# Fused linear attention and MoE block on one core: MoE groups of four chunks, with the second weight stationary and the output kept transposed

## The chip, the core and the metric

The kernel runs on one core of one Trainium2 chip. The metric is device time in microseconds (us), from the launch of the one program to its end. Lower is better. The kernel before takes 521.38 us, the median of three runs (520.69 to 521.63). Arrays are rearranged on the host before and after the program; that is not in the time.

## The reference, cut to what matters

Two stages follow each other. The first is a linear attention with a decaying state, over 4 batches, 8 heads, 768 time steps and a head dimension of 48:

```
cur = (u * k_t) outer v_t
y_t = r_t @ (state + cur)
state = w_t * state + k_t outer v_t
```

Its output is read as `x`, 3072 tokens by 384. The second stage is a two-layer network with 2048 hidden units:

```
h = x @ w_in                                      # 3072 x 2048
g = max(h, 0) + alpha * min(h, 0)
out = g @ w_out                                   # 3072 x 384
```

Everything is single precision in and out. The weights arrive as 64-bit numbers and are turned into single precision on the chip.

## The kernel before, in words

**Chunks.** Time is cut into 12 pieces of 64 steps, and batches are taken in pairs, so there are 24 chunks of 128 tokens, q = 0 to 23. For each chunk VectorE (DVE) runs two scans over the decay `w` and scales `k` and `r`; TensorE (PE) forms scores, the output of the chunk and the update of the state in many 64x64 matmuls; the result goes to `x` in two parts, a rounded high part and the low remainder, so that three fast matmuls (high x high, high x low, low x high) give close to single precision. A quarter of the rows of `x` comes out on other partitions, in a tile `x3s`, and six small DMAs per group (L614) move it to its place.

**Weights.** There are 16 tiles of 128 hidden units, j = 0 to 15. Each tile is read from memory as 64-bit numbers (`raw<-in_wts_dram`, L647, 768 KB, into one of two `raw` buffers), put together by DVE (L659, L662, L666), split into `wh` and `wl`, and stays in SBUF. The tiles used in the first steps keep their `w_out` half whole at first; it goes to `wl` by a DMA (`wl<-cx`, L631).

**MoE steps.** Chunks are joined in groups of 2, 2, 3, 3, 3, 3, 3, 3 and 2 (`GROUPS`). One step is one group with one weight tile: `moe_up` (L691) issues 9 matmuls (three parts of K, three products) with 128 hidden units as stationary and the tokens of the group moving, 256 or 384 columns; ScalarE (ACT) and DVE make `g` from the sum (L697, L699) and split it into `gh` and `gl` (L704, L705); `moe_down` of the step two before (`LAG = 2`) then issues, for each chunk of the group, three matmuls with the chunk's 128 columns of `g` as stationary and 384 columns of `w_out` moving (L719). Each chunk has its own accumulator in PSUM, a tile `op`, of which there are three. In the first 24 steps `g` isn't split: one exact single-precision product (L713), which the chip runs as two passes, takes the place of the three.

**Order at the start.** Attention must yield chunks and the weights must be read before the matmuls can run. So the first two groups of two chunks take turns over the weight tiles: tiles 0 to 5 with group 0, then with group 1, then tiles 6 to 10 with each, then 11 to 15 with each (`PHASES`). When a group is left, its unfinished sums are written to memory (`part<-os`, L746), and read back and added by DVE (L735, L737) when it is taken up again.

**What sets the order.** All operations are first recorded with an engine, a duration, what they read and write, and a due time. A planner (`Plan.order`) then plays the engines forward and gives each the ready operation with the earliest due time; the program is emitted in that order, and each engine and SyncE's (SP) one DMA queue run it strictly in that order. `LEAD`, `UNIT`, `ATT`, `PLACE` and `PLACE_REST` set the due times: at which step each chunk's attention is wanted.

**The end.** When a group is done, the sums of each chunk are copied from PSUM to one of two `os` tiles by ACT or DVE (L743, L740) and written with two DMAs (L751). A check that the fast path was allowed runs beside it; its result, `flag`, is read by every engine before a branch.

Of the kernel before, what the change touches and what calls it, by code (L numbers as in the profile page):

```python
# [8 lines left out]
F32 = mybir.dt.float32  # L9
# [24 lines left out]
GT = 3 * P  # L34
# [14 lines left out]
LEAD = 22.0  # L49
UNIT = 1.05  # L50
ATT = 2.9

PLACE = {0: (-1, -1), 1: (4, 5)}
PLACE_REST = (12, 7, 3)
# [3 lines left out]
WHOLE_TO = 24  # L58
# [3 lines left out]
CHECK_FROM = 52  # L62
# [163 lines left out]
def fast_path(tc, wgt, flag, dmaj, nat, u, ud, vg, wts, alpha, out, part):  # L226
# [12 lines left out]
    with tc.tile_pool(name="const", bufs=1) as const, tc.tile_pool(name="psum", bufs=1, space=PSUM) as psum:  # L239
# [36 lines left out]
        r_x = ring("x", [P, 2, KT, GT], 3, F32R)  # L276
# [4 lines left out]
        r_os = ring("os", [P, DM], 2)  # L281
# [6 lines left out]
        def warm():  # L288
            return tmp.ap[:, 2 * P:]
# [32 lines left out]
        group, starts = [], []  # L322
        for g, size in enumerate(GROUPS):
            starts.append(len(group))
            group += [(g, i) for i in range(size)]
        begins, first, sizes = [], {}, []
        for g, j0, j1 in PHASES:
            first.setdefault(g, len(sizes))
            begins.append(len(sizes))
            sizes += [GROUPS[g]] * (j1 - j0)  # L330
        steps = len(sizes)
        before = {}
        for q, (g, i) in enumerate(group):
            before.setdefault(PLACE[g][i] if g in PLACE else first[g] - PLACE_REST[i], []).append(q)
# [3 lines left out]
        for i in range(steps + 5):  # L338
            for q in before.get(i, ()):
                due_att[q] = now  # L340
                now += ATT
            due_step.append(now)
            now += UNIT * (sizes[i] if i < steps else 3)

# [4 lines left out]
        def load(q):  # L349
# [11 lines left out]
            if q < GROUPS[0]:  # L361
                op("SP", 0.4, lambda: nc.sync.dma_start(out=extra[q].ap, in_=vg[q]), w=[extra[q]], lat=0.55)
# [101 lines left out]
        def outputs(q, nxt):  # L464
# [5 lines left out]
            g, s = group[q]  # L470
            size = GROUPS[g]
            kr, nv, at = ready.pop(q)
            ss = slice(s * P, (s + 1) * P)
            if s == 0:
                xs[g] = Tensor(r_x), Tensor(r_x3) if g > 0 else None
            x, xr = xs[g]
            yb = Tensor(r_op if g == 0 else bank), Tensor(bank)
# [13 lines left out]
            def own(same):  # L491
# [3 lines left out]
                for j in range(2):  # L495
                    for o, e in ORDER:
                        i, p = o if same else 1 - o, 2 * j + e
                        h = o * NP + p
                        if g > 0 or 2 * o + j < KT:
                            made.append(mm(yb[o], FULL[e], col(j, i), not same, lhsT=nv.ap[FULL[i], h * 64:(h + 1) * 64],  # L500
                                           rhs=at.ap[FULL[i], o, p, :]))
                if g == 0:
# [67 lines left out]
            if g == 0:  # L570
# [34 lines left out]
            take(g > 0)  # L605
            if g > 0 and nxt:
                rest()
            if g > 0 and s == size - 1:
                src = [(xr, (i, j, 1)) for i in range(size) for j in range(2)]
                old = [(x, (i, j, o)) for i in range(size) for j in range(2) for o in range(2)]  # L610
                for e in range(2):
                    for k in range(KT):
                        def move(r=64 * e + D, f=64 * e + 16 * k, k=k):
                            nc.sync.dma_start(out=x.ap[r:r + 16, :, k, 0:size * P].bitcast(F32), in_=xr.ap[f:f + 16, :, 0:size * P].bitcast(F32))  # L614
                        op("SP", 0.4, move, r=src + old, w=[(x, ("d", e, k))], lat=0.15)

        def x_keys(g):
            x = xs[g][0]
            return [(x, (i, j, o)) for i in range(GROUPS[g]) for j in range(2) for o in range(2)] + (
                [(x, ("d", o, k)) for o in range(2) for k in range(KT)] if g > 0 else [])  # L620


        whole = {j for i, (g, j0, j1) in enumerate(PHASES) for j in range(j0, j1) if begins[i] + j - j0 < WHOLE_TO}
# [19 lines left out]
        def weight_tile(j):  # L643
# [5 lines left out]
            for i0, i1 in ((0, 1), (1, 2)) if j < SPLIT else ((0, 2),):  # L649
# [15 lines left out]
                if j in whole:  # L665
# [15 lines left out]
        def moe_up(n, g, j, lag):  # L681
            x, w = xs[g][0], GROUPS[g] * P
            us = lambda t: t * (0.25 + 0.25 * GROUPS[g])
            hp, pos = Tensor(bank), Tensor(r_pos)

            def products():
                i = 0
                for k in range(KT):
                    ks = slice(k * P, (k + 1) * P)
                    for a, xi in ((wh, 0), (wl, 0), (wh, 1)):  # L690
                        nc.tensor.matmul(hp.ap[:, 0:w], lhsT=a[:, j, 0, ks], rhs=x.ap[:, xi, k, 0:w],  # L691
                                         start=(i == 0), stop=(i == 3 * KT - 1))
                        i += 1
            t = UNIT * GROUPS[g]
            op("PE", t / 2, products, r=[("wh", j, 0), ("wl", j, 0), ("down", n - lag - 1), *x_keys(g)], w=[hp, "up"], kind="MM",
               due=due_step[n] + t / 2 - (t if n == steps - 1 else 0))
            op("ACT", us(0.6), lambda: nc.scalar.activation(out=pos.ap[:, 0:w], in_=hp.ap[:, 0:w], func=AF.Relu, scale=alpha_n[:, j:j + 1]),  # L697
               r=[hp, "alpha"], w=[pos])
            op("DVE", us(0.58), lambda: nc.vector.scalar_tensor_tensor(  # L699
                out=pos.ap[:, 0:w], in0=hp.ap[:, 0:w], scalar=0.0, in1=pos.ap[:, 0:w], op0=ALU.max, op1=ALU.subtract), r=[hp], w=[pos])  # L700
            if n < WHOLE_TO:
                return pos, None
            gh, gl = Tensor(r_gh), Tensor(r_gl)
            op("ACT", us(0.54), lambda: nc.scalar.copy(out=gh.ap[:, 0:w], in_=pos.ap[:, 0:w]), r=[pos], w=[gh])  # L704
            op("DVE", us(0.6), lambda: nc.vector.tensor_tensor(out=gl.ap[:, 0:w], in0=pos.ap[:, 0:w], in1=gh.ap[:, 0:w].bitcast(F32), op=ALU.subtract),  # L705
# [3 lines left out]
        def moe_down(n, g, j, lag, gh, gl, j0, j1):  # L709
            size = GROUPS[g]  # L710
            for s in range(size):
                def whole_products(s=s):
# [359 lines left out]
```

## Time and profile before

| | |
|---|---|
| median of three runs | 521.38 us (520.69 to 521.63) |
| the profiled execution | 520.97 us, of which 519.2 us is the span of the trace |
| instructions in the span | 13761 |
| PE busy, DVE busy, ACT busy | 501.7 us, 345.6 us, 300.3 us |
| matmuls of `moe_up` | 1296 (864 + 432) |
| matmuls of `moe_down`, in three products | 1008 (3 x 336) |
| passes of exact `moe_down` | 96 |
| PE's granted clock, mean | 0.996 |

A row of the grouped view names line, engine, operation, output tile, then input tiles (the moving one first for a matmul), its shape and count, the busy time and the mean duration of one, and the idle time of the engine before them with what ended it. Matmuls overlap in their pipeline, so the duration of one (some 0.3 us) is longer than the spacing from one to the next; the spacing is read from the chain of waits, whose rows give start, length and number of a run of matmuls. Busy times of DVE and ACT count overlapping time once.

### The profile page before, as it was taken

The numbers are of one execution on the slowest core, as the hardware profiler recorded it, in microseconds if no ns is written. First come the engines' busy times: TensorE is split into PE (matmuls) and PEld (weight loads), VectorE is DVE, ScalarE is ACT, GpSimd is POOL, SyncE is SP. The second block draws the span as 40 slices with busy tenths as digits, with TensorE's granted clock in tenths as the row PEclk, the third lists the DMA queues.
The fourth block names the chain that finished last, engine by engine and source line by source line (L and its number), as shares of the span: only waits on it lengthen the run. The fifth ranks groups of instructions, "written<-read, shape, count | busy, mean of one in ns | idle before, by whom it ended". The sixth has DMA issues, their size and how long they took to land.

```text
span 519.2 us, 13761 instructions
## 1 busy us (share of the span) xinstructions
PE 501.7 (97%) x5654; PEld 473.4 (91%) x5654; DVE 345.6 (67%) x657; ACT 300.3 (58%) x806; POOL 74.4 (14%) x100
## 2 busy tenths in 40 slices
PE   9996899999999999999999999999999999999993
PEld 8984677789999999999999999999999999999992
DVE  6989798998888898768336665676753434433341
ACT  3765754865354576756555566676775656533441
POOL 2010120262001544213000210102000000000000
PEclk9999999999999999999999999999999999999998
DMA  8878768765231668465413556447461045000101
GB/s 300 277 263 286 235 237 283 257 204 151 78 104 33 220 197 271 121 194 157 113 59 103 177 159 208 139 145 228 126 227 61 15 120 180 7 12 16 33 1 37
DMA packets 31945, 78.27 MB, mean 151 GB/s; under 512 B 4480, under 2 KB 13184, under 8 KB 31872
## 3 DMA queue, kind: packets, MB, share of 16 engines
q1 hardware_dynamic: 31872, 77.30, 46.6%
q8 instruction: 46, 0.75, 0.6%
q14 instruction: 27, 0.22, 0.1%
HBM read 66.27 MB, written 6.29 MB: 140 GB/s over the span
## 4 chain that ended last, share of the span: by engine, by line
PE 85%; DMA 8%; DVE 3%; SPq 1%; ACT 1%; issue 1%; POOL 0%; DVEq 0%; POOLq 0%
PE bank L691 36%; PE op L719 32%; PE bank L483 5%; PE op L713 5%; DMA raw<-in_wts_dram 4%; DMA wl<-cx 3%; PE bank L440 2%; PE bank L458 1%; PE bank L527 1%; PE bank L758 1%; SPq L614 1%; PE bank L766 1%; PE bank L401 1%; DVE cx L662 0%; DVE cx L666 0%
## 5 line engine op out<-in xcount | busy, mean ns | idle before, releaser
L691 PE MATMUL bank<-x,wh 128*128 128x384 f32 (+1 forms) x864 | 230.2, 328 | 0.3 <-ACT cd L404 0.3
L691 PEld LDWEIGHTS bank<-x,wh 128*128 128x128 f32 x864 | 153.3, 188 | 5.2 <-issue 0.8
L697 ACT ACTIVATE pos<-bank,alpha_n 128x384 f32<-128x384 f32 (+1 forms) x144 | 78.4, 545 | 104.0 <-PE bank L691 103.8
L691 PE MATMUL bank<-x,wl 128*128 128x384 f32 (+1 forms) x432 | 137.0, 317 | 0.0
L699 DVE SCALAR_TENSOR_TENSOR pos<-bank,pos 128x384 f32<-128x384 f32 (+1 forms) x144 | 73.5, 511 | 86.8 <-ACT pos L697 86.2
L719 PE MATMUL op<-wh,gl 128*128 128x384 f32 x336 | 112.6, 335 | 0.3 <-DVE gl L705 0.2
L719 PE MATMUL op<-wh,gh 128*128 128x384 f32 x336 | 112.9, 336 | 0.0
L719 PE MATMUL op<-wl,gh 128*128 128x384 f32 x336 | 112.4, 335 | 0.0
L705 DVE TENSOR_TENSOR gl<-pos,gh 128x384 fp32r<-128x384 f32 (+1 forms) x120 | 68.0, 567 | 51.2 <-ACT gh L704 50.6
L691 PEld LDWEIGHTS bank<-x,wl 128*128 128x128 f32 x432 | 81.4, 188 | 2.1
L704 ACT CAST gh<-pos 128x384 fp32r<-128x384 f32 (+1 forms) x120 | 58.7, 489 | 38.0 <-DVE pos L699 37.7
L719 PEld LDWEIGHTS op<-wh,gl 128*128 128x128 f32 x336 | 63.2, 188 | 1.1 <-DVE gl L705 1.1
L719 PEld LDWEIGHTS op<-wh,gh 128*128 128x128 f32 x336 | 63.2, 188 | 0.6 <-ACT gh L704 0.4
L719 PEld LDWEIGHTS op<-wl,gh 128*128 128x128 f32 x336 | 63.1, 188 | 0.0
L416 ACT ACTIVATE at<-ident,cd 128x64 f32<-128x64 f32 x192 | 53.4, 342 | 6.0 <-PE bank L483 5.2
L426 POOL TENSOR_TENSOR St<-St,pc_all 128x192 f32<-128x192 f32 x44 | 27.4, 637 | 203.2 <-DVE St L603 113.9
L713 PE MATMUL op<-wl,pos 128*128 128x384 f32 x96 | 35.9, 492 | 5.7 <-DMA wl<-cx 4.2
L408 POOL TENSOR_TENSOR rk<-rk,u_bc 128x384 f32<-128x384 f32 x18 | 20.8, 1156 | 123.3 <-DMA rk<-in_nat_dram 93.4
L378 DVE TENSOR_TENSOR_SCAN suf<-wd,low 128x528 f32<-128x528 f32 x23 | 30.4, 1321 | 4.3 <-DMA wd<-in_dmaj_dram 4.3
L384 DVE TENSOR_TENSOR_SCAN wd<-wd,low 128x528 f32<-128x528 f32 x23 | 28.8, 1252 | 0.1
L713 PEld LDWEIGHTS op<-wl,pos 128*128 128x128 f32 x96 | 16.3, 190 | 13.1 <-DVE kr L390 2.5
L445 DVE COPY_PREDICATED at<-mask,bank 128x256 f32<-128x256 int32 x48 | 19.2, 441 | 8.6 <-PE bank L527 7.2
(107 smaller groups left out, 538.0 us busy)
## 6 DMA issues: line engine op xcount, KB each, us to landing
raw<-in_wts_dram SPq DMA_DIRECT2D x32, 768.0 KB, 5.2
kr<-in_dmaj_dram SPq DMA_DIRECT2D x24, 512.0 KB, 4.5
rk<-in_nat_dram SPq DMA_DIRECT2D x18, 384.0 KB, 3.6
raw<-in_dmaj_dram SPq DMA_DIRECT2D x12, 528.0 KB, 4.4
nv<-in_nat_dram SPq DMA_DIRECT2D x24, 256.0 KB, 4.3
wd<-in_dmaj_dram SPq DMA_DIRECT2D x23, 264.0 KB, 3.9
out_dram<-os SPq DMA_DIRECT2D x46, 96.0 KB, 2.2
wl<-cx SPq DMA_DIRECT2D x13, 192.0 KB, 4.9
```

The source lines that it names most:

```text
L378: op("DVE", 1.28, lambda: nc.vector.tensor_tensor_scan(out=suf.ap[:, ::-1], data0=wv()[:, ::-1], data1=low[:, ::-1], initial=0.0, op0=ALU. ...
L384: op("DVE", 1.28, lambda: nc.vector.tensor_tensor_scan(out=wv(), data0=wv(), data1=low, initial=0.0, op0=ALU.mult, op1=ALU.max), r=["low"] ...
L416: nc.scalar.activation(out=at.ap[:, o, p, :], in_=ident2, func=AF.Copy, scale=cd.ap[:, o * NP + p:o * NP + p + 1])
L426: op("POOL", 0.5, lambda i=i: nc.gpsimd.tensor_tensor(out=St[m][:, i, :, 0:D], in0=St[m][:, i, :, 0:D], in1=pc_all[:, q, i::2].unsqueeze(2 ...
L483: last[0] = nc.tensor.matmul(t.ap[rows, cols], start=(t, rows.start) not in open_, stop=stop, skip_group_check=True, **kw)
L691: nc.tensor.matmul(hp.ap[:, 0:w], lhsT=a[:, j, 0, ks], rhs=x.ap[:, xi, k, 0:w], start=(i == 0), stop=(i == 3 * KT - 1))
L697: op("ACT", us(0.6), lambda: nc.scalar.activation(out=pos.ap[:, 0:w], in_=hp.ap[:, 0:w], func=AF.Relu, scale=alpha_n[:, j:j + 1]), r=[hp, ...
L699: op("DVE", us(0.58), lambda: nc.vector.scalar_tensor_tensor(out=pos.ap[:, 0:w], in0=hp.ap[:, 0:w], scalar=0.0, in1=pos.ap[:, 0:w], op0=AL ...
L704: op("ACT", us(0.54), lambda: nc.scalar.copy(out=gh.ap[:, 0:w], in_=pos.ap[:, 0:w]), r=[pos], w=[gh])
L705: op("DVE", us(0.6), lambda: nc.vector.tensor_tensor(out=gl.ap[:, 0:w], in0=pos.ap[:, 0:w], in1=gh.ap[:, 0:w].bitcast(F32), op=ALU.subtrac ...
L713: nc.tensor.matmul(ops_[s].ap[:, 0:DM], lhsT=gh.ap[:, s * P:(s + 1) * P], rhs=wl[:, j, 1, :].bitcast(F32), start=(j == j0), stop=(j == j1 ...
L719: nc.tensor.matmul(ops_[s].ap[:, 0:DM], lhsT=a.ap[:, ts], rhs=w[:, j, 1, :], start=(j == j0 and i == 0), stop=(j == j1 - 1 and i == 2))
```

## The change: what it does

**Groups.** All groups have four chunks (`GS = 4`), so there are six. A whole step moves 512 tokens in `moe_up`, one full PSUM bank. The first six weight tiles of groups 0 and 1 are done in halves, chunks 0 and 1 of the group first, then chunks 2 and 3 (`HALVES`, `steps_of`), and all later tiles with the four chunks together. There are 108 steps in place of 144.

**Down.** The 128 x 128 blocks of `w_out` are now stationary and `gh` or `gl` moves, 512 columns (256 in a half step). The sums come out transposed: three accumulators for the three blocks of 128 output columns, each 512 tokens wide, so again three `op` banks. The order of the three products is now (`wh`, `gh`), (`wl`, `gh`), (`wh`, `gl`). Nothing is written to memory between: a group is finished before the next begins, so the writes, the reads and DVE's additions of `part` are gone.

**Output.** The program writes the transposed result, 384 x 3072, and the host turns it. Each group has three writes of 128 x 512; the last group has six of 128 x 256, its banks being copied out in halves by ACT and DVE at once.

**Also.** Exact products are used for weight tiles 0 to 11 of group 0 (18 steps in place of 24); `x` has two buffers in place of three, each wider; a group in halves has its six row moves per half; due times and planned durations are changed. The path for inputs that the fast one can't take is rewritten to the same output layout; it isn't run here.

```diff
-GROUPS = (2, 2, 3, 3, 3, 3, 3, 3, 2)
-PHASES = [(g, j0, j1) for j0, j1 in ((0, 6), (6, 11), (11, NF)) for g in range(2)] + [(g, 0, NF) for g in range(2, len(GROUPS))]
+NG = NQ // GS
+HALVES = (6, 6) + (0,) * (NG - 2)
+def steps_of(g):
+    n = HALVES[g]
...
+        early = [(g, j, 0, 2) for j in range(n)] + [(g, j, 2, 4) for j in range(n)]
+    return early + [(g, j, 0, GS) for j in range(n, NF)]
+STEPS = [x for g in range(NG) for x in steps_of(g)]
-LEAD = 22.0
-UNIT = 1.05
-ATT = 2.9
-PLACE = {0: (-1, -1), 1: (4, 5)}
-PLACE_REST = (12, 7, 3)
+LEAD = 20.0
+ATT = 2.7
+PLACE = {0: (-1, -1, 4, 5), 1: (-7, -4, 3, 5)}
+PLACE_REST = (-13, -10, -6, -3)
...
-        r_x = ring("x", [P, 2, KT, GT], 3, F32R)
+        r_x = ring("x", [P, 2, KT, GT], 2, F32R)
...
+            for s0, s1 in spans(g):
+                if s != s1 - 1:
+                    continue
...
-                            nc.sync.dma_start(out=x.ap[r:r + 16, :, k, 0:size * P].bitcast(F32), in_=xr.ap[f:f + 16, :, 0:size * P].bitcast(F32))
+                            nc.sync.dma_start(out=x.ap[r:r + 16, :, k, cs].bitcast(F32), in_=xr.ap[f:f + 16, :, cs].bitcast(F32))
...
+        def spans(g):
+            return ((2, 4),) if g == 0 else ((0, 2), (2, 4)) if HALVES[g] else ((0, GS),)
...
-            for s in range(size):
-                def products(s=s):
-                    for i, (a, w) in enumerate(((gh, wh), (gl, wh), (gh, wl))):
-                        nc.tensor.matmul(ops_[s].ap[:, 0:DM], lhsT=a.ap[:, ts], rhs=w[:, j, 1, :], start=(j == j0 and i == 0),
-                                         stop=(j == j1 - 1 and i == 2))
+            for k in range(KT):
+                def products(k=k, ks=ks):
+                    for i, (a, b) in enumerate(((wh, gh), (wl, gh), (wh, gl))):
+                        nc.tensor.matmul(ops_[k].ap[:, cs], lhsT=a[:, j, 1, ks], rhs=b.ap[:, 0:w], start=(begin and i == 0),
+                                         stop=(end and i == 2), skip_group_check=True)
...
-                if j0 > 0:
-                    op("SP", 0.4, lambda q=q, os_=os_: nc.sync.dma_start(out=os_.ap, in_=part[q]), r=[("part", q)], w=[os_],
-                       lat=0.6, due=due_step[n] - 2.0)
-                    op("DVE", 0.58, lambda s=s, os_=os_: nc.vector.tensor_tensor(out=os_.ap, in0=ops_[s].ap[:, 0:DM], in1=os_.ap, op=ALU.add),
-                       r=[ops_[s]], w=[os_], due=due_step[n] + 3.0)
...
+                halves = ((0, GT // 2), (GT // 2, GT)) if last else ((0, GT),)
...
+                    op("SP", 0.4, lambda k=k, os_=os_, a=a, b=b: nc.sync.dma_start(
+                        out=out[k * P:(k + 1) * P, g * GT + a:g * GT + b], in_=os_.ap[:, a:b]), r=[(os_, h)],
+                       w=[("out", g, k, h)], lat=0.8, due=due_step[n] + 11.0)
...
-_OUTS = [((B * S, DM), 'float32')]
+_OUTS = [((DM, B * S), 'float32')]
```

The planner makes of this another order on every engine. Three places matter for what follows.

The first place is SP's DMA queue in the first stretch of the program, around the six moves that complete `x` for chunks 2 and 3 (`x<-x3s`; `raw` are weight tiles, `wl<-cx` their whole `w_out` halves, `kr`, `nv`, `wd` the inputs of later chunks). Before:

```order
L647 DMA raw_98<-in_wts_dram 128x1536
L631 DMA wl<-cx_99 128x384
L631 DMA wl<-cx_100 128x384
L647 DMA raw_97<-in_wts_dram 128x1536
L353 DMA wd_102<-in_dmaj_dram 128x528
L631 DMA wl<-cx_99 128x384
L647 DMA raw_98<-in_wts_dram 128x1536
L614 DMA x_117<-x3s_119 16x2x256 x6
L647 DMA raw_97<-in_wts_dram 128x1536
```

And now:

```order
L673 DMA raw_97<-in_wts_dram 128x1536
L374 DMA kr_102<-in_dmaj_dram 128x1024
L380 DMA nv_107<-in_nat_dram 128x512
L373 DMA wd_101<-in_dmaj_dram 128x528
L673 DMA raw_96<-in_wts_dram 128x1536
L657 DMA wl<-cx_99 128x384
L657 DMA wl<-cx_98 128x384
L673 DMA raw_97<-in_wts_dram 128x1536
L637 DMA x_115<-x3s_117 16x2x256 x6
```

Before, the moves are preceded by 8 loads of weight tiles from the program's start, now by 10.

The second place is PE in the middle of the program, a step's second part (`moe_down`), each row one matmul with the moving operand named first. Before, for the three chunks of a group:

```order
L719 MATMUL op_72<-wh,gh_126 128x384
L719 MATMUL op_72<-wh,gl_128 128x384
L719 MATMUL op_72<-wl,gh_126 128x384
L719 MATMUL op_73<-wh,gh_126 128x384
L719 MATMUL op_73<-wh,gl_128 128x384
```

Now, for the three blocks of output columns:

```order
L751 MATMUL op_73<-gh_122,wh 128x512
L751 MATMUL op_73<-gh_122,wl 128x512
L751 MATMUL op_73<-gl_126,wh 128x512
L751 MATMUL op_71<-gh_122,wh 128x512
L751 MATMUL op_71<-gh_122,wl 128x512
```

There are nine such matmuls to a step in both, each with its own stationary block; they now move 512 columns, and a step serves four chunks.

The third place is the end of DVE's queue. It now reads:

```order
L726 SCALAR_TENSOR_TENSOR pos_118<-bank_76,pos_118 128x512
L875 CAST flag<-bank_74 1x1
L732 TENSOR_TENSOR gl_126<-pos_118,gh_124 128x512
L771 COPY os_128<-op_73 128x256
L771 COPY os_127<-op_71 128x256
L771 COPY pos_119<-op_72 128x256
```

The copy of `flag` stands ahead of the last `gl`. The matmul that it reads (L873) stands on PE ahead of the last step's nine down matmuls. Before, that copy had 26 more instructions of the fast path behind it on DVE, and the matmul had 12 `moe_up` steps behind it on PE. On SP, in both, the read of `flag` stands ahead of the last group's writes.

More of the change, by code (lines that the diff above doesn't have):

```diff
@@ L61 @@
 U_BY_PE = 6
-CHECK_FROM = 52
 LO_BY_PE = 6
@@ L223, in order, with fast_path @@
         return sorted((o for o in ops if o.start is not None), key=lambda o: (o.start, o.n))
-def fast_path(tc, wgt, flag, dmaj, nat, u, ud, vg, wts, alpha, out, part):
+def fast_path(tc, wgt, flag, dmaj, nat, u, ud, vg, wts, alpha, out):
     nc = tc.nc
@@ L319, in fast_path, with mm_time, up_time, down_time @@
         op("ACT", 0.2, lambda: nc.scalar.mul(out=alpha_n, in_=alpha_n, mul=-1.0), r=["alpha"], w=["alpha"])
[L322 to L331, printed above, removed]
+        steps = len(STEPS)
+        whole = [g == 0 and j < WHOLE for g, j, c0, c1 in STEPS]
+        first = {}
+        for n, (g, j, c0, c1) in enumerate(STEPS):
+            first.setdefault(g, n)
+        def mm_time(w, exact=False):
+            return 2 * (2 * w + 6) / 2400 if exact else 3 * (w + 32) / 2400
+        def up_time(n):
+            g, j, c0, c1 = STEPS[n]
+            return KT * mm_time((c1 - c0) * P)
+        def down_time(n):
+            g, j, c0, c1 = STEPS[n]
+            return KT * mm_time((c1 - c0) * P, whole[n])
         before = {}
-        for q, (g, i) in enumerate(group):
-            before.setdefault(PLACE[g][i] if g in PLACE else first[g] - PLACE_REST[i], []).append(q)
+        for q in range(NQ):
+            g, i = divmod(q, GS)
+            at = PLACE.get(g, PLACE_REST)[i]
+            before.setdefault(at if g == 0 else first[g] + at, []).append(q)
         due_att, due_step, now = {}, [], LEAD
@@ L697, in moe_up @@
-            op("ACT", us(0.6), lambda: nc.scalar.activation(out=pos.ap[:, 0:w], in_=hp.ap[:, 0:w], func=AF.Relu, scale=alpha_n[:, j:j + 1]),
+            t = up_time(n)
+            op("PE", t, products, r=[("wh", j, 0), ("wl", j, 0), ("down", n - LAG - 1), *x_keys(g, c0, c1)], w=[hp, "up"], kind="MM",
+               due=due_step[n] + t - (2 * t if n == steps - 1 else 0))
+            op("ACT", us(0.52), lambda: nc.scalar.activation(out=pos.ap[:, 0:w], in_=hp.ap[:, 0:w], func=AF.Relu, scale=alpha_n[:, j:j + 1]),
@@ L999, in body @@
         )
-        part = dram.tile([NQ, P, DM], F32, name="part")
         xd = dram.tile([B, S, HD], F32, name="xd")
-        fast_path(tc, wgt, flag, dmaj, nat, u, ud, vg, wts, alpha, out, part)
+        fast_path(tc, wgt, flag, dmaj, nat, u, ud, vg, wts, alpha, out)
         good = nc.values_load(flag, min_val=0, max_val=P)
```

229 lines of the change are left out of this document (117 added, 112 removed).

## The prediction

> **What bounds the kernel now.** I read the page's engine shares and chain first, then the busy time by stretch, then the chain row by row for the spacing of matmuls, then the start and the end.
>
> ```profile
> span 519.2 us, 13761 instructions
> PE 501.7 (97%) x5654; PEld 473.4 (91%) x5654; DVE 345.6 (67%) x657; ACT 300.3 (58%) x806; POOL 74.4 (14%) x100
> PE 85%; DMA 8%; DVE 3%; SPq 1%; ACT 1%; issue 1%; POOL 0%; DVEq 0%; POOLq 0%
> ```
>
> The third row is the chain that ended last: 85% of it is PE. The three stretches below (start to the first group of three chunks, from there to the last up step, the end) show busy time of PE, PEld, DVE, ACT and POOL:
>
> ```profile
> 4.30:128.50 124.20, 117.07 (x1491) 97.78 (x1491) 112.82 (x196) 77.55 (x221) 24.17 (x24) 1.00 0.76 255
> 128.50:507.20 378.70, 378.21 (x4138) 369.98 (x4137) 231.37 (x459) 219.76 (x581) 47.06 (x56) 1.00 0.39 120
> 507.20:519.20 12.00, 3.18 (x17) 2.38 (x15) 1.41 (x3) 1.36 (x3) 0.00 (x0) 0.80 0.18 40
> ```
>
> In the middle PE is idle 0.5 of 378.7 us while DVE has 39% free: there only the length of the matmul stream counts. In the first stretch DVE is busy 112.8 of 124.2 us and DMA 76%: chunks and weight tiles set the pace there, and PE's share includes waiting inside matmul records. The last 12 us are a tail.
>
> **The stream.** Spacings come from the chain, whose rows give start, length and number of matmuls:
>
> ```profile
> 68.98 1.29 PE op L713 x4
> 385.61 1.56 PE bank L691 x9
> 387.17 1.56 PE op L719 x9
> 505.21 1.04 PE op L719 x6
> 506.26 1.07 PE bank L691 x9
> ```
>
> So 384 columns take 1.56/9 = 173.3 ns, up or down alike; 256 columns 1.07/9 = 118.9 ns; a pass of the exact product 1.29/4 = 322.5 ns for 384. The counts (up, three products down of which one row is shown, exact):
>
> ```profile
> L691 PE MATMUL bank<-x,wh 128*128 128x384 f32 x576 | 165.1, 340 | 0.0
> L691 PE MATMUL bank<-x,wl 128*128 128x384 f32 x288 | 96.4, 335 | 0.0
> L691 PE MATMUL bank<-x,wh 128*128 128x256 f32 x288 | 65.1, 302 | 0.3 <-ACT cd L404 0.3
> L691 PE MATMUL bank<-x,wl 128*128 128x256 f32 x144 | 40.6, 282 | 0.0
> L719 PE MATMUL op<-wh,gh 128*128 128x384 f32 x336 | 112.9, 336 | 0.0
> L713 PE MATMUL op<-wl,pos 128*128 128x384 f32 x96 | 35.9, 492 | 5.7 <-DMA wl<-cx 4.2
> ```
>
> Before: 864 + 1008 of 384 columns are 324.4 us, 432 of 256 are 51.4, 96 exact passes 31.0: together 406.8 us. After, from the step table: 24 half steps and 84 whole ones give 216 ups of 256 and 756 of 512; downs in three products are 108 of 256 and 702 of 512; exact ones are 72 passes of 256 and 36 of 512. At 0.84 ns a column the exact ones are again 31.0 us; the 324 of 256 columns are 38.5. The rest are 1458 of 512 columns, a width that no row shows. The exact pass streams 768 column times in 322.5 ns, 0.42 ns each; that leaves 11.4 ns of fixed part at 256 and 12.0 at 384. So I take 215.0 + 12.3 = 227.3 ns, which is 331.4 us. The sum after is 400.9, a gain of **5.9 us**. No work is saved: 1782 such instructions in place of 2304 pay the fixed part of some 12 ns 522 times less. Bounds: no fixed part at all, 215.0 ns, gains 17.9 us more; in proportion to 384, 231.1 ns, gains 5.5 us less.
>
> The Trainium skill's page "TensorE: Matmul & The Clock Gate" (Back-to-back issue gap) gives N/2.4 + 2.5 ns when warm. That would be 162.5 ns at 384 columns against the trace's 173.3 and 215.8 ns at 512; the trace disagrees at both widths it shows, so the rows' fixed part stands here and the page's figure is only a rival.
>
> **What leaves the path at no gain.** The eight writes and eight reads of partial sums, and DVE's eight additions (0.55 us each), leave the first stretch; ACT and DVE work per column falls a little, since each instruction is wider. In the middle DVE and ACT have cover (231 and 220 of 379 us); without it nothing of the stream would be gained. Two `x` buffers in place of three cost nothing: the first chunk of a group is wanted 13 steps before it, when the buffer has been free for 3.
>
> **The start.** The first up step of chunks 2 and 3 needs the six moves, and SP's queue now holds ten weight loads ahead of them, not eight. SP's own rows of the start:
>
> ```profile
> 41.24 0.33 SPq L647 DMA_DIRECT2D raw<-in_wts_dram  x1
> 51.87 0.96 SPq L647 DMA_DIRECT2D raw<-in_wts_dram  x1
> 53.79 4.02 SPq L614 DMA_DIRECT2D x<-x3s  x6
> 57.91 0.53 SPq L647 DMA_DIRECT2D raw<-in_wts_dram  x1
> 60.90 0.48 SPq L647 DMA_DIRECT2D raw<-in_wts_dram  x1
> 67.19 0.34 SPq L647 DMA_DIRECT2D raw<-in_wts_dram  x1
> ```
>
> The tenth load was issued at 60.90, after the moves had held the queue for 4.02 us. So the moves would now start between 57.4 (60.90 + 0.48 - 4.02) and 61.4, which is 3.6 to 7.6 us later than 53.79; I take the middle, 5.6, because the tiles' pace is set partly by the queue and partly by DVE. Behind the moves on SP stand the eleventh load and the `w_out` copy; PE waits, since its order is fixed. Part comes back. PE does the outputs of one chunk more ahead of this step:
>
> ```profile
> 107.31 1.32 PE bank L483 x80
> ```
>
> which for all 96 matmuls of a chunk is 1.6 us moved, not added. And soon after this step PE waited for a tile that now is already there:
>
> ```profile
> 64.63 0.91 PE L713 MATMUL op<-wl,pos 128*128 128x384 f32 x2 [1.28 <-DVE pos L699]
> ```
>
> So the start costs 5.6 - 1.6 - 1.3 = **2.7 us**; bounds -1.3 (moves as early as before, the wait gone) and 6.0 (7.6 - 1.6).
>
> **The end.** Wider tiles lengthen the last chain from the last up to the last down:
>
> ```profile
> L697 ACT ACTIVATE pos<-bank,alpha_n 128x384 f32<-128x384 f32 x96 | 55.7, 581 | 75.0 <-PE bank L691 75.0
> L699 DVE SCALAR_TENSOR_TENSOR pos<-bank,pos 128x384 f32<-128x384 f32 x96 | 53.3, 556 | 70.2 <-ACT pos L697 69.9
> L704 ACT CAST gh<-pos 128x384 fp32r<-128x384 f32 x96 | 48.9, 510 | 29.8 <-DVE pos L699 29.5
> L697 ACT ACTIVATE pos<-bank,alpha_n 128x256 f32<-128x256 f32 x48 | 22.7, 473 | 29.0 <-PE bank L691 28.9
> L699 DVE SCALAR_TENSOR_TENSOR pos<-bank,pos 128x256 f32<-128x256 f32 x48 | 20.2, 421 | 16.5 <-ACT pos L697 16.4
> L704 ACT CAST gh<-pos 128x256 fp32r<-128x256 f32 x24 | 9.8, 408 | 8.3 <-DVE pos L699 8.2
> ```
>
> Going on in a straight line to 512 columns, the three are 0.69 + 0.69 + 0.61 = 1.99 us, and some 0.3 between engines: `gh` is there 2.3 us after the last up. The nine downs of the step before cover 2.05 of it, so PE waits about 0.25. The last `gl` stands behind the copy of `flag` on DVE, which waits for a matmul behind those nine downs; it ends near 3.1 us after the last up where the third matmul wants it at 2.75: 0.35 more. Together 0.6, where now stand 0.21 and 0.27:
>
> ```profile
> 508.79 0.19 PEld L719 LDWEIGHTS op<-wh,gh 128*128 128x128 f32 x1 [0.21 <-ACT gh L704]
> 509.25 0.19 PEld L719 LDWEIGHTS op<-wh,gl 128*128 128x128 f32 x1 [0.27 <-DVE gl L705]
> 510.06 0.34 PE L719 MATMUL op<-wl,gh 128*128 128x384 f32 x1
> 510.41 1.11 SPq L751 DMA_DIRECT2D out_dram<-os  x2
> 511.62 1.74 SPq L751 DMA_DIRECT2D out_dram<-pos  x2
> ```
>
> That is +0.1. SP took 2.95 us to issue four writes (510.41 to 513.36), the first right after the last matmul. Six at 0.55 to 0.87 each are 3.3 to 5.2 us, but the first bank is ready 1.36 us before the last matmul ends. Bounds -0.7 and +1.2; I take +0.4. The end costs **0.5 us**.
>
> **Sum.** -5.9 + 2.7 + 0.5 = -2.7. The profiled execution took 520.97 us for its 519.2 of span, 0.4 under the median of 521.38; so 518.3 for such an execution, and 521.38 - 2.7 = **518.7 us** for the median.
>
> **Rivals.** *The start is not late*: the two extra tiles go through in gaps, because DVE is rid of the additions and the queue of the partial sums. For it: SP was held 4.02 us by the moves, near to what two loads take. Against: DVE is 91% busy there, and its queue now has two more tiles ahead of the step. -5.9 - 1.3 + 0.5 gives 514.7.
>
> *The start eats it all*, the side of slower: each weight tile takes its full period ahead of the moves, (67.19 - 41.24)/5 = 5.2 us, as the two `raw` buffers must be emptied by DVE in turn. Two are 10.4 - 1.6 = 8.8 us, nothing comes back: -5.9 + 8.8 + 0.5 = +3.4, 524.8. It decides once the moves start later than about 61 us. Against it: the moves' own 4 us lie in that period.
>
> *The wide matmul costs in proportion*, 231.1 ns: -2.7 + 5.5, 524.2. Against it: the fixed part grew by only 0.6 ns from 256 to 384.
>
> *Group ends*: there are two `os` buffers for three banks, so the third copy waits until the first write has landed, some 4 us; where PE's order leaves less between, each of five ends costs about 0.7 us, 3.5 in all: 522.2, no change to be measured. The chain shows no such wait now, with three chunks and the same two buffers.
>
> *The change streams at the page's gap*: at 215.8 ns the stream is 16.8 us shorter, 501.9 us.
>
> **How the numbers follow.** Forecast 0.51, of which 0.08 within 0.2% of before (about what a measurement of this kernel can tell from no change); start not late 0.17; start eats all 0.13; proportion 0.06; group ends 0.09; the page's gap 0.04. Faster is 0.43 + 0.17 + 0.04 = 0.64; same is 0.08 + 0.09 = 0.17; slower 0.19. The range reaches from 514.0, the early start with a little more, to 523.5, most of the two slower cases left out. The forecast's own range is 516 to 520.5.
>
> **What would show it.** Right: nine 512-column matmuls in 2.05 us; the moves between 57 and 61 us; the middle without idle PE; the end about 14 us after the last up (12.0 now, plus 1.5 for 18 wide downs in place of 15, plus 0.5). Wrong: matmul spacing outside 225 to 230 ns; the first up step of chunks 2 and 3 before 60 or after 67 us (before: 58.1); waits of PE for `os` or an accumulator at group ends; DVE or ACT as releaser in the middle.
>
> ```profile
> 58.12 0.36 PE L691 MATMUL bank<-x,wh 128*128 128x256 f32 x1
> ```

## The result and the profile after

The changed kernel takes 528.24 us (median; 525.36 to 528.93), where the kernel before takes 521.5 us beside it: a ratio of 1.012, with a 95% interval of 1.0079 to 1.0162. It is slower by 1.2%. The prediction was 518.7 us, with a range to 523.5. The profiled execution took 527.59 us, with a span of 525.8.

First the rows of the page: span, busy time of the engines, PE's clock in 40 slices of 13.1 us, and the shares of the chain that ended last.

```profile
span 525.8 us, 12462 instructions
PE 498.4 (95%) x5140; PEld 415.8 (79%) x5140; DVE 334.2 (64%) x581; ACT 286.0 (54%) x737; POOL 75.2 (14%) x100
PEclk9999889999999999999999999999999999999997
PE 87%; DMA 6%; ACT 2%; DVE 2%; issue 1%; SPq 1%; POOL 0%; ACTq 0%; POOLq 0%
```

PE is busy 3.3 us less than before (501.7), and the span is 6.6 us longer: PE stands still for 27.4 us, 9.9 more than before. The lower clock in slices five and six (52 to 79 us) is new. Where it waits shows in busy time by stretch; the columns are the stretch, its length, then busy time and instructions of PE, PEld, DVE, ACT and POOL, PE's granted clock, DMA share and GB/s.

```profile
4.30:128.50 124.20, 113.13 (x1251) 92.57 (x1251) 107.66 (x173) 70.58 (x193) 21.12 (x22) 0.97 0.67 224
128.50:180.00 51.50, 46.23 (x933) 43.22 (x932) 42.83 (x90) 34.02 (x111) 14.90 (x18) 1.00 0.63 202
180.00:511.00 331.00, 330.89 (x2929) 273.65 (x2928) 181.03 (x314) 177.49 (x427) 35.99 (x41) 1.00 0.35 107
511.00:525.80 14.80, 4.93 (x21) 3.12 (x19) 2.62 (x6) 2.33 (x5) 0.00 (x0) 0.78 0.19 60
```

From 180 us to the last up step PE is idle 0.1 of 331 us, group ends included. The loss lies in two places: ahead of 128.5 us, where PE was busy 117.1 us before and now 113.1, and in the 51.5 us behind it, where PE stands still for 5.3 (0.1 before). The stream itself came out as predicted. The chain shows it, here with the last up step and the downs behind it:

```profile
509.12 2.04 PE bank L718 x9
511.16 2.04 PE op L751 x9
```

2.04 / 9 = 226.7 ns for 512 columns, up and down alike (227.3 were assumed).

**The start.** The chain of waits between 54 and 73 us, in order of time (start, length, what):

```profile
54.28 6.40 DMA raw<-in_wts_dram
...
60.76 0.14 ACT raw L683
...
61.55 0.37 ACT x L584
...
66.91 1.99 DMA x<-x3s
...
68.94 3.42 PE bank L718 x15
```

The chain goes through a raw weight tile, but not because the first up step of chunks 2 and 3 needs that tile. ACT works in order, and the instruction that waits for it (L683) stands ahead of the casts of these chunks' low parts (L584). The same stretch of the timelines of PE, DVE, ACT and SP shows what else is late; the last column is the idle time before an instruction and what ended it:

```profile
48.56 0.94 PE L503 MATMUL bank<-nv,kn 64*64 64x48 f32 x29
56.89 0.35 DVE L623 TENSOR_TENSOR St<-bank,St 128x192 f32<-128x192 f32 x1
57.16 0.95 DVE L692 CUSTOM_DVE_ANT_0 cx<-raw,cx 128x1536 uint16<-128x1536 uint16 x1
58.03 0.88 DVE L623 TENSOR_TENSOR St<-bank,St 128x192 f32<-128x192 f32 x3
58.43 0.33 PE L580 MATMUL bank<-x,minus 128*128 128x128 f32 x1 [0.75 <-DVE St L623]
58.72 0.53 SPq L673 DMA_DIRECT2D raw<-in_wts_dram  x1
60.76 0.89 ACT L683 ACTIVATE raw<-raw 128x768 int32<-128x768 uint32 x1 [2.11 <-DMA raw<-in_wts_dram]
61.55 0.80 ACT L584 CAST x<-bank 128x256 fp32r<-128x256 f32 x3
62.88 5.27 SPq L637 DMA_DIRECT2D x<-x3s  x6
```

In the kernel before the same places read (the attention of chunk 3, the state additions, the casts):

```profile
36.24 0.98 PE L483 MATMUL bank<-nv,kn 64*64 64x48 f32 x30
51.18 0.88 DVE L603 TENSOR_TENSOR St<-bank,St 128x192 f32<-128x192 f32 x3
52.47 0.80 ACT L564 CAST x<-bank 128x256 fp32r<-128x256 f32 x3
```

Everything on the way to the six moves is later by 7 to 12 us: chunk 3's attention by 12.3, the additions that bring the state of chunks 2 and 3 up to date by 6.8 (the last three of them, 58.03 against 51.18), the casts by 9.1, the moves by 9.1 (53.79 before). The last additions now stand on DVE behind nine instructions that finish a weight tile or half of one (L692, the ninth at 57.16); before, they stood behind seven (L666). That is two more tiles. So 6.8 us of the casts' delay of 9.1 come with the additions; the other 2.2 are ACT's wait for the raw tile and its work on it (L683). The additions read the banks into which PE then subtracts the high part (L580), so PE waits for them. SP's queue is not what holds the moves: the tenth weight load went out at 58.72, earlier than before (60.90), and SP then had nothing to issue for 3.6 us.

**Group 1.** Two rows of PE's timeline, with two of ACT's between them:

```profile
158.79 0.35 PE L718 MATMUL bank<-x,wh 128*128 128x256 f32 x1 [2.10 <-DMA x<-x3s]
167.11 0.73 ACT L842 ACTIVATE raw<-raw,m_one 128x528 f32<-128x528 f32 x1 [3.73 <-DMA raw<-in_dmaj_dram]
167.85 0.39 ACT L731 CAST gh<-pos 128x256 fp32r<-128x256 f32 x1
169.11 0.28 PE L751 MATMUL op<-gh,wh 128*128 128x256 f32 x1 [2.95 <-issue]
```

Chunks 6 and 7, in halves, wait for their moves, and soon after for the split of their hidden values. That split starts late because ACT works in order: DVE had the hidden values ready at 165.7 us (L726, 165.28 and 0.41 long), but the cast L731 stood behind an instruction of the check (L842) that waited for its transfer, and started at 167.85. So some 2.1 of the 2.95 us have the same kind of cause as ACT's wait at the start. The kernel before has no wait of PE of such a length between 100 and 200 us.

### The profile page after: what moved, and what is told of

The parts are those of the page before. It is cut to its first block, busy times and chain, and to the rows that moved or that the text cites. A ratio compares the mean times of both kernels' runs of the same rounds, so it can differ in the third digit from the quotient of the medians.

```text
span 525.8 us, 12462 instructions
## 1 busy us (share of the span) xinstructions
PE 498.4 (95%) x5140; PEld 415.8 (79%) x5140; DVE 334.2 (64%) x581; ACT 286.0 (54%) x737; POOL 75.2 (14%) x100
## 4 chain that ended last, share of the span: by engine, by line
PE 87%; DMA 6%; ACT 2%; DVE 2%; issue 1%; SPq 1%; POOL 0%; ACTq 0%; POOLq 0%
PE bank L718 37%; PE op L751 33%; DMA raw<-in_wts_dram 5%; PE bank L503 5%; PE op L746 5%; PE bank L460 2%; PE bank L478 1%; PE bank L781 1%; PE bank L547 1%; DMA x<-x3s 1%; PE bank L789 1%; ACT at L436 1%; ACT raw L683 1%; SPq L637 1%; DVE cx L692 1%
## 5 line engine op out<-in xcount | busy, mean ns | idle before, releaser
L718 PE MATMUL bank<-x,wh 128*128 128x512 f32 (+1 forms) x648 | 205.5, 376 | 4.9 <-DMA x<-x3s 4.6
L726 DVE SCALAR_TENSOR_TENSOR pos<-bank,pos 128x512 f32<-128x512 f32 (+1 forms) x108 | 68.0, 630 | 123.8 <-ACT pos L724 123.4
L724 ACT ACTIVATE pos<-bank,alpha_n 128x512 f32<-128x512 f32 (+1 forms) x108 | 69.2, 641 | 131.9 <-PE bank L718 131.6
L718 PE MATMUL bank<-x,wl 128*128 128x512 f32 (+1 forms) x324 | 119.1, 367 | 0.2 <-DVE wl L662 0.2
L751 PE MATMUL op<-gh,wh 128*128 128x512 f32 (+1 forms) x270 | 103.6, 384 | 3.0 <-issue 3.0
L751 PE MATMUL op<-gl,wh 128*128 128x512 f32 (+1 forms) x270 | 101.5, 376 | 0.1
L751 PE MATMUL op<-gh,wl 128*128 128x512 f32 (+1 forms) x270 | 101.3, 375 | 0.0
L732 DVE TENSOR_TENSOR gl<-pos,gh 128x512 fp32r<-128x512 f32 (+1 forms) x90 | 64.3, 715 | 32.0 <-ACT gh L731 30.1
L731 ACT CAST gh<-pos 128x512 fp32r<-128x512 f32 (+1 forms) x90 | 53.0, 590 | 34.4 <-DVE pos L726 33.8
L751 PEld LDWEIGHTS op<-gh,wl 128*128 128x128 f32 x270 | 50.9, 188 | 11.7 <-issue 3.0
```

What stands on the lines that cost most here:

```text
L724: op("ACT", us(0.52), lambda: nc.scalar.activation(out=pos.ap[:, 0:w], in_=hp.ap[:, 0:w], func=AF.Relu, scale=alpha_n[:, j:j + 1]), r=[hp, ...
L726: op("DVE", us(0.5), lambda: nc.vector.scalar_tensor_tensor(out=pos.ap[:, 0:w], in0=hp.ap[:, 0:w], scalar=0.0, in1=pos.ap[:, 0:w], op0=ALU ...
L731: op("ACT", us(0.48), lambda: nc.scalar.copy(out=gh.ap[:, 0:w], in_=pos.ap[:, 0:w]), r=[pos], w=[gh])
L732: op("DVE", us(0.55), lambda: nc.vector.tensor_tensor(out=gl.ap[:, 0:w], in0=pos.ap[:, 0:w], in1=gh.ap[:, 0:w].bitcast(F32), op=ALU.subtract),
L751: nc.tensor.matmul(ops_[k].ap[:, cs], lhsT=a[:, j, 1, ks], rhs=b.ap[:, 0:w], start=(begin and i == 0), stop=(end and i == 2), skip_group_c ...
```

## The experiments

All times are medians; the ratio is to the kernel before, run beside each. The last column is the start of the six moves of chunks 2 and 3 in the profile.

| run | us | ratio, 95% interval | moves start |
|---|---|---|---|
| kernel before | 521.2 to 522.5 | 1 | 53.79 |
| changed kernel | 528.24 | 1.012 (1.0079 to 1.0162) | 62.88 |
| state additions early | 516.64 | 0.9911 (0.9883 to 0.9939) | 55.43 |
| group 1 in whole steps | 513.12 | 0.9846 (0.9802 to 0.9891) | 56.99 |
| more fillers | 528.80 | 1.0123 (1.0079 to 1.0166) | 63.47 |
| chunks 2, 3 before step 3 | 519.28 | 0.9947 (0.9923 to 0.9971) | 55.60 |
| group 1 placed earlier | 520.61 | 0.9984 (0.9964 to 1.0003) | 61.09 |
| before, additions early | 520.44 | 0.9989 (0.9968 to 1.0009) | 47.82 |
| chunks 2, 3 before step 4 | 532.84 | 1.0242 (1.0212 to 1.0273) | 72.61 |
| whole steps and step 3 | 515.40 | 0.9885 (0.9858 to 0.9912) | 56.58 |
| landing 1.3 us later in the plan | 512.07 | 0.9798 (0.9751 to 0.9845) | 48.70 |
| that, and whole steps | 509.27 | 0.9753 (0.9707 to 0.9798) | 49.04 |
| before, landing later | 520.34 | 0.9974 (0.9952 to 0.9996) | 49.07 |

**1. The state additions early.**

```diff
-  out=St..., in0=uv(), in1=St..., op=ALU.add), r=[ub[i]], w=[(f"St{m}", i)])
+  out=St..., in0=uv(), in1=St..., op=ALU.add), r=[ub[i]], w=[(f"St{m}", i)], due=due_att[q] + 2.0)
```

> One thing differs from the changed kernel: the four additions on DVE that bring the state of chunks 2 and 3 up to date get an early due time of their own. Theory A (order): in the changed kernel DVE does them at 56.9 to 58.9 us behind two weight tiles, the low part of these chunks waits for their banks, and so the six moves start at 62.9 us. Then here the moves start before 58 us, the first up step of chunks 2 and 3 before 63 us (68.1 before), and the time falls by 4 to 8 us, to 520 to 524. Theory B (two more tiles): the moves are late because two more weight tiles have to go through DMA, DVE and ACT ahead of them; the additions come early, but PE then waits for tiles instead, the four chunks' up steps end within 1 us of 127.4 us, and the time stays within 1.5 us of 528.2.

Measured: 516.64 us, 11.6 less. Theory A, by more than it said. The additions of chunk 3 now stand at 52.2 us, and the moves go out ahead of the weight load of 59.56, the ninth; in the changed kernel the ninth and the tenth went first. SP's and DVE's timelines:

```profile
52.19 0.62 DVE L623 TENSOR_TENSOR St<-bank,St 128x192 f32<-128x192 f32 x2
55.43 4.00 SPq L637 DMA_DIRECT2D x<-x3s  x6
59.56 0.50 SPq L673 DMA_DIRECT2D raw<-in_wts_dram  x1
```

Busy time by stretch, first this kernel, then the changed one:

```profile
60.00:80.00 20.00, 19.04 (x224) 16.77 (x221) 16.10 (x29) 10.66 (x22) 2.33 (x3) 1.00 0.78 271
140.00:160.00 20.00, 19.86 (x359) 18.97 (x350) 17.76 (x39) 12.73 (x42) 2.16 (x4) 1.00 0.65 199
160.00:180.00 20.00, 20.00 (x349) 17.61 (x348) 18.64 (x37) 14.65 (x46) 7.45 (x9) 1.00 0.47 150
```

```profile
60.00:80.00 20.00, 15.45 (x196) 14.48 (x197) 14.84 (x25) 10.83 (x31) 3.70 (x4) 0.83 0.70 237
140.00:160.00 20.00, 17.68 (x440) 16.57 (x431) 16.42 (x39) 13.60 (x48) 1.96 (x4) 1.00 0.45 136
160.00:180.00 20.00, 17.05 (x362) 16.40 (x361) 16.70 (x34) 13.92 (x48) 10.77 (x12) 1.00 0.80 277
```

The idle time of group 1 is gone as well, though nothing there was edited. An early due time changes the whole order behind it, so this run shows that the lost time is a matter of order; it doesn't price the additions alone.

**2. Group 1 in whole steps.**

```diff
-HALVES = (6, 6) + (0,) * (NG - 2)
+HALVES = (6, 0) + (0,) * (NG - 2)
-PLACE = {0: (-1, -1, 4, 5), 1: (-7, -4, 3, 5)}
+PLACE = {0: (-1, -1, 4, 5)}
```

> Only group 0 keeps its six steps in halves; group 1 (chunks 4 to 7) goes in whole steps of 512 columns from its first step, its chunks placed like those of the later groups. Theory A: the halves put chunks 6 and 7 so late that PE waits for their moves (156 to 159 us) and for the split behind them (166 to 169 us), 5.6 us in all; here both waits are gone, and the time is 521 to 524 us with the start as it was. Theory B: between 130 and 180 us DVE has too much to do in any order; then the waits only move to the first whole step of group 1, and the time stays within 1.5 us of 528.2.

Measured: 513.12 us, 15.1 less. PE is busy 30.0 of 30 us from 150 to 180. But "with the start as it was" was wrong: the moves went out at 56.99, since here too the order of the start changed. So this is no price of the halves alone. One sum fits well: with 12 half steps the stream is 1566 matmuls of 512 columns at 226.7 ns, 108 of 256 at 118.9 and the same exact passes, 398.9 us against 406.8 before, 7.9 less; the kernel is 8.1 us faster than the one before. With no net loss at the start, the change would be worth about what its stream saves; but the sum leaves out the end, so part of the fit may be luck.

**3. More fillers.**

```diff
-FILL, FILL_FROM, FILL_TO = 80, 6.0, 60.0
+FILL, FILL_FROM, FILL_TO = 160, 6.0, 74.0
```

> As the changed kernel, but the filler matmuls that keep PE busy while it has nothing else to do may be put in until 74 us of the plan instead of 60: some nine pairs more, between 63 and 70 us. Theory clock: after PE's idle time the granted clock is 0.58 in 68 to 72 us, and that is why the eighteen matmuls of the first up step take 4.1 us instead of 2.1; with the fillers the clock there is 0.9 or more, the eighteen take 2.2 us or less, and the time falls by 1.5 to 2.5 us though work is added. Theory feed: the eighteen are slow because something feeds them late (weights, moves); then they take 4 us still, and the time is the same within 0.7 us or longer.

Measured: 528.80 us, no change. The clock part of the first theory holds, its gain doesn't. Of the changed kernel, busy time and clock in four stretches that follow each other, and in a later one:

```profile
58.38:61.79 3.41, 1.28 (x7) 0.97 (x7) 1.59 (x5) 1.30 (x3) 0.60 (x2) 1.00 0.94 328
61.79:65.20 3.41, 3.24 (x110) 3.15 (x110) 3.41 (x7) 2.96 (x10) 1.37 (x2) 0.50 0.37 128
65.20:68.61 3.41, 1.08 (x22) 0.74 (x19) 3.41 (x6) 1.12 (x4) 0.00 (x0) 1.00 0.16 34
68.61:72.03 3.42, 3.15 (x15) 3.09 (x15) 1.33 (x3) 0.87 (x2) 0.00 (x0) 0.50 0.77 205
167.60:171.01 3.41, 1.90 (x16) 1.90 (x16) 2.88 (x5) 2.83 (x12) 1.13 (x2) 1.00 0.91 324
```

The granted clock changes at the borders of the first four, 3.41 us apart. It falls at 61.79, inside PE's wait of 2.24 us, and again at 68.61, when the wait of 2.23 us has been over for half a microsecond and the first three matmuls have run at full clock. It stays full behind PE's waits of 1.83, 2.10 and 2.95 us (ahead of 55.23, 158.79 and 169.11); the last row holds the end of the longest.

With the fillers, PE's timeline (twenty filler matmuls, the three parts of the attention behind them, twelve more fillers, the first matmul of the up step, the filler behind its nine):

```profile
63.60 4.63 PE L789 MATMUL bank<-ident 128*128 128x128 f32 x20
68.17 0.70 PE L503 MATMUL bank<-nv,kn 64*64 64x48 f32 x32
...
70.09 1.60 PE L789 MATMUL bank<-ident 128*128 128x128 f32 x12
71.46 0.36 PE L718 MATMUL bank<-x,wh 128*128 128x256 f32 x1
...
72.61 0.61 PE L789 MATMUL bank<-ident 128*128 128x128 f32 x4
```

The nine matmuls of the up step now take 1.15 us (71.46 to 72.61), 128 ns each; in the changed kernel's chain fifteen of them took 3.42, 228 each (both with the longer start of the first one). The slow first up step was the clock's doing, not late data. But the fillers themselves ran at half clock, 228 ns each (63.60 to 68.17) in place of 114 later (70.09 to 71.46), and PE's order is fixed: the attention stood behind 4.6 us of them, and the up step began 3.4 us later. Fillers put in after the clock has fallen pay for its recovery with the time they were to save.

**4. Chunks 2 and 3 before step 3.**

```diff
-PLACE = {0: (-1, -1, 4, 5), 1: (-7, -4, 3, 5)}
+PLACE = {0: (-1, -1, 3, 3), 1: (-7, -4, 3, 5)}
```

> As the changed kernel, but the attention of chunks 2 and 3 is placed before step 3 (both) instead of before steps 4 and 5, so that DVE makes the features of chunk 3 ahead of a weight tile. Theory A (order): the moves start before 59 us, the first up step of chunks 2 and 3 before 64 us, and the time falls by 3 to 7 us. Theory B (two more tiles): what the attention gains the tiles lose, PE waits for tiles before 58 us, and the time stays within 1.5 us of 528.2.

Measured: 519.28 us, 9.0 less, the moves at 55.60. Theory A, again by more than it said.

**5. Group 1 placed earlier.**

```diff
-PLACE = {0: (-1, -1, 4, 5), 1: (-7, -4, 3, 5)}
+PLACE = {0: (-1, -1, 4, 5), 1: (-8, -5, -2, 1)}
```

> As the changed kernel, but the attention of chunks 4 to 7 is placed 8, 5 and 2 steps ahead of group 1 and one step behind its start, instead of 7 and 4 ahead, 3 and 5 behind; the start of the program is left as it is (moves of chunks 2 and 3 at 62 to 64 us). Theory placement: chunks 6 and 7 were put too late; the waits of PE at 156 to 159 and 166 to 169 us go, and the time falls by 4 to 6 us, to 522 to 524. Theory knock-on: PE waits in group 1 because DVE and ACT are behind ever since the late start; then as much idle time shows elsewhere between 130 and 200 us, and the time stays within 1.5 us of 528.2.

Measured: 520.61 us, 7.6 less, with the start nearly as late as in the changed kernel (moves at 61.09). Busy time by stretch:

```profile
60.00:80.00 20.00, 16.78 (x202) 15.23 (x203) 16.89 (x29) 10.53 (x26) 3.25 (x5) 0.83 0.79 268
160.00:180.00 20.00, 20.00 (x248) 18.43 (x247) 18.97 (x37) 12.99 (x37) 4.38 (x5) 1.00 0.43 133
```

The low clock and the idle time at 60 to 80 us are still there; that of 160 to 180 is gone, and from 140 to 160 us PE was busy 19.9 of 20 us. So the waits of group 1 do not need a cause at the start: an earlier place for chunks 4 to 7 is enough, and the time doesn't come up elsewhere. Theory placement, with a gain somewhat above the 5.3 us of idle time; the moves came 1.8 us earlier too, which may be part of it.

**6. The kernel before, with the additions early.** The edit of the first experiment, in the kernel before.

> The kernel before, with the same early due time for the four state additions on DVE that took 11.6 us off the changed kernel. Theory A (the late additions are what the change brought with it): in the kernel before they came at 50.0 to 52.0 us and the moves at 53.8 were not what PE waited for longest, so here the moves may start up to 4 us earlier, but the time stays within 1.5 us of 521.2. Theory B (the additions are late in any kernel of this kind, and the gain of the first experiment is not the change's loss given back): 3 us or more come off here too, 518 or less.

Measured: 520.44 us, a ratio of 0.9989: no change that can be told. Theory A in its time, though not quite in its reason: the moves came 6 us earlier, and PE was busy 22.5 us of the 24 from 36 to 60 us where it had been busy 18.8. Part of the gain was given back at 128 us, by a new wait for moves, with a low clock behind it (0.91 in the mean of 120 to 140 us); the row of PE's timeline:

```profile
130.34 0.41 PE L691 MATMUL bank<-x,wh 128*128 128x384 f32 x1 [2.25 <-DMA x<-x3s]
```

**7. Chunks 2 and 3 before step 4**, the suspected delay made larger.

```diff
-PLACE = {0: (-1, -1, 4, 5), 1: (-7, -4, 3, 5)}
+PLACE = {0: (-1, -1, 4, 4), 1: (-7, -4, 3, 5)}
```

> As the changed kernel, but with the attention of chunks 2 and 3 both placed before step 4 instead of before steps 4 and 5, which by the order worked out puts the second part of the attention of chunk 3 behind more work of the tiles: the suspected delay made larger. Theory A (what counts is when the six moves can start): the moves start at 70 us or later, the first up step of these chunks after 75 us, and the time grows by 4 to 10 us, to 532 to 538. Theory B (tiles set the pace of the first stretch): DVE uses the time for tiles, PE catches up before 130 us, and the time stays within 2 us of 528.2.

Measured: 532.84 us, 4.6 more; the moves at 72.61. Theory A. A further delay of 9.7 us costs only 4.6: about half comes back later.

**8. Whole steps and step 3 together**, the edits of the second and the fourth.

> The edits of the second and the fourth experiment together: group 1 in whole steps from its first one, and the attention of chunks 2 and 3 both before step 3. Theory one cause: each of the two edits by itself already brought the moves to 55 to 57 us, so together they gain no more than the better one: 511 to 515 us. Theory two causes: the two gains (15 and 9 us) add up at least in part: 509 or less.

Measured: 515.40 us, 2.3 more than with whole steps alone. That is just above the range of one cause (511 to 515). The two gains don't add up, which fits one cause at the start that either edit removes.

**9. The landing of a raw tile 1.3 us later in the plan.**

```diff
-   w=[(raw, 0), (raw, 1)], lat=2.2)
+   w=[(raw, 0), (raw, 1)], lat=3.5)
```

> As the changed kernel, but the planner takes 1.3 us more for the landing of a raw weight tile (the trace shows 4.5 to 7.2 us from issue to landing, median 5.1). No instruction is added or taken away, only the order of each engine can move. Theory A (order, now on ACT): in the changed kernel the low-part casts of chunks 2 and 3 stood on ACT behind the first instruction on a raw tile that had not landed, 2.1 us of waiting; with a later landing in the plan they stand ahead of it, the moves start before 58 us, and the time falls by 8 to 12 us, to 516 to 520, as when only the state additions were put early. Theory B (the additions on DVE are the only cause): the moves stay at 61 us or later and the time within 2 us of 528.2.

Measured: 512.07 us, 16.2 less, beyond theory A's range. The number enters only into the order; every instruction is still there. The plan had a raw tile land 4.6 us after its issue began (0.4 for the issue, 2.0 for any transfer, 2.2 here) or later; in the changed kernel the tile of 54.28 us took 6.40. The row of landings in the changed kernel, then DVE, ACT and SP here:

```profile
DMA to landing us min/median/max: 4.5/5.1/7.2
```

```profile
45.50 1.14 DVE L623 TENSOR_TENSOR St<-bank,St 128x192 f32<-128x192 f32 x4
47.35 0.82 ACT L584 CAST x<-bank 128x256 fp32r<-128x256 f32 x3 [0.73 <-PE bank L580]
48.70 3.37 SPq L637 DMA_DIRECT2D x<-x3s  x5
52.84 0.96 ACT L683 ACTIVATE raw<-raw 128x768 int32<-128x768 uint32 x1 [0.90 <-DMA raw<-in_wts_dram]
```

The additions, the casts and the moves all stand ahead of the tile that ACT waits for, and the moves come 14.2 us earlier than in the changed kernel. This run moves DVE's and ACT's order together, so it doesn't say how the loss divides between them; that stays open. Nor is all of it the start's: from 128.5 to 180 us PE is busy 49.6 of 51.5 us here, against 46.2 in the changed kernel.

**10. That edit with whole steps.** The edits of the second and the ninth experiment.

> Group 1 in whole steps, as in the second experiment, and the planned landing of a raw tile 1.3 us later. In the second experiment ACT waited 2.15 us for a raw tile ahead of the low-part casts, PE stood 2.4 us behind that, and the granted clock fell. Theory A: that wait goes, 2 to 4 us come off the 513.1 us: 509 to 511. Theory B: the first stretch is then bound by the work of DVE and the landing of tiles, what is won before 60 us is lost before 130 us, and the time stays within 1.5 us of 513.1.

Measured: 509.27 us, theory A; the fastest kernel of all, 2.5% under the kernel before.

**11. The kernel before with the later landing.** The edit of the ninth experiment, in the kernel before.

> The kernel before, with the planned landing of a raw weight tile 1.3 us later, the edit that took 16 us off the changed kernel. Theory A (the changed order lost what this gives back): in the kernel before the low-part casts of chunks 2 and 3 stood on ACT at 52.5 to 53.8 us without a tile ahead of them that had not landed, so the time stays within 2 us of 521.5, and between two kernels that both have the edit the change is worth 8 to 10 us. Theory B (the plan's landing time costs every kernel of this kind): 6 us or more come off here as well, 515 or less, and the change is worth only the stream's 6 to 7 us or less.

Measured: 520.34 us, a ratio of 0.9974: a gain of a quarter of a per cent, half a per cent at most by the interval. Theory A. With the edit in both, the change is worth 512.07 against 520.34, 8.3 us; with the additions early in both (first and sixth experiment) it is 516.64 against 520.44, 3.8 us.

## Why the prediction was wrong

**The stream: right.** 226.7 ns for 512 columns, where 227.3 were taken: 1458 x 226.7 = 330.5, in all 400.0 us, a gain of 6.8 against the predicted 5.9. The rivals of a matmul in proportion (231.1 ns) and of a gap of 215.8 ns fell. The formula on the Trainium skill's page "TensorE: Matmul & The Clock Gate" (Back-to-back issue gap) is off by 11 ns at this width too; the page calls it that of an isolated matmul, and its figure for a sustained stream at 512 columns, about 131 ns, is further off still.

**The middle and the group ends: right.** From 180 us on PE is idle 0.1 us; no wait for `os` at any group end.

**The start: the step that failed.** "SP's queue now holds ten weight loads ahead of them, not eight ... so the moves would now start between 57.4 and 61.4." They started at 62.88, and PE's first up step of chunks 2 and 3 at 68.08, past the 67 that the prediction named as the mark of its own failure. The mechanism was wrong more than the size. SP had no loads to issue when the moves came; they waited for their data, which ACT, PE and DVE made late because the planner's new order puts two more tiles ahead of the state additions on DVE, and on ACT a tile that had not landed ahead of the casts. The prediction treated the start as a queue with two more entries; it is an order, and five edits of placement, due time, half steps or planned landing (experiments 1, 2, 4, 8 and 9), none of which takes a tile out of the program, bring the moves to between 48.7 and 57.0 us. The return of 1.3 us came: the timeline shows no wait of PE between 72 and 130 us. But the term had no place for PE's halved clock, which took more than that back. The order of the changed kernel could be read ahead of the run: state additions, casts and tiles stand in it in just this sequence on DVE and ACT. The prediction took its term from SP alone, though it noted under a rival that DVE's queue has two more tiles ahead of the step.

**Group 1: not in the sum at all.** The prediction costed the halves only by their matmul counts. PE stood still for 5.3 us between 128.5 and 180, and the fifth experiment gives 7.6 us for the placement alone. "The middle without idle PE" held only from 180 us.

**The end: its mechanism right.** The last up step ends at 511.16 by the chain, 14.6 us ahead of the end, where about 14 were predicted. In the kernel before it is 11.9 us by the chain, so the end cost some 1.3 us beyond the 1.5 of the wider downs, where 0.5 was put. SP took 6.2 us for the six writes (3.3 to 5.2 were given), as its last rows show:

```profile
515.09 2.54 SPq L773 DMA_DIRECT2D out_dram<-os  x3
...
519.20 2.13 SPq L773 DMA_DIRECT2D out_dram<-pos  x1
```

The rival "the start eats it all" named the point from which it decides, moves later than 61 us, and that point was reached; but its reason, two whole tile periods ahead of the moves, is only half right: both loads went out earlier than before, while DVE did finish two more tiles ahead of the additions. Its chance of 0.13 was too low because placement, which the change rewrites for both groups in halves, was taken as given.

The sum, as far as it can be made: the stream gives 6.8 back, and the kernel is 6.7 us slower, so 13.5 us are lost. The two profiles account for nearly all of it. PE stands still 3.9 us longer up to 128.5 us (11.1 against 7.1), 5.2 longer from there to 180 us and 1.1 longer at the end. It also works 6.4 us at the halved clock (3.24 and 3.15 us), which by an estimate would be 3.2 at the full one. So the start cost about 7 us (3.9 + 3.2) in place of 2.7, group 1 about 5 in place of nothing, and the end about 1 in place of 0.5. No run gives a price for DVE's order and for ACT's wait apart. Of the delay of the moves DVE's order is the larger part: in the second experiment ACT still waits 2.15 us ahead of the casts, but the additions stand at 51.59 us, and the moves come 5.9 us earlier than in the changed kernel. Two edits that only reorder recover 11.6 and 16.2 us, the second more than was lost: PE's idle time is 15.9 us there, against 17.5 in the kernel before.

## What to carry to other kernels

Where a planner or a list of due times orders the work, a change of sizes is also a change of order; read the new order on every engine that feeds the first late step, not only on the one that issues it. An in-order engine that waits for a load makes everything behind it wait, so 1.3 us in a planned landing, which moved the time by 16.2 us in one kernel and by little over 1 in the other, can count for more than a wider matmul gains. And compare two kernels in more than one order: here the change looked 1.2% slower, and with the same ordering edit in both it is worth 0.7% (3.8 us) or 1.6% (8.3 of 520.3 us).

## What the runs showed of the hardware

In the changed kernel the granted clock changes at 61.79, 65.20, 68.61 and 72.03 us, each some 3.41 us after the last (10.24 us for three steps), and these times are not those at which PE's waits begin or end. What PE does between two such borders counts, not the length of one wait: the clock fell behind stretches in which PE was busy 1.28 and 1.08 us (the rows of the third experiment), and stayed full behind one of 1.90, although PE's wait of 2.95 us ends in it; 31 such steps after 61.79, at 167.60, a border would cut that wait in two, an estimate from the first four. In the kernel before PE waited 2.33 us ahead of the exact products at 47.90 us and then ran at full clock. Busy time isn't the whole rule: in the seventh experiment the clock fell at 49.96 us, though PE was busy 2.52 of the 3.41 us ahead of it. What else counts, no run here shows. What the fall costs is on record: the starts of nine matmuls of 256 columns from 69.54 to 71.46 us lie 213 ns apart, in place of 119.

The Trainium skill's page "TensorE: Matmul & The Clock Gate" (What's actually happening) has the clock fall after an idle window of 3.4 us and lets that window run freely, whatever the kernel does. The length of the window and its running freely agree with the borders 3.41 us apart. "Idle" can't mean without work: PE was busy 1.28 and 1.08 us in the two windows ahead of the falls.
